# Spectral stage with four input buffers and tables per iteration, hd turned in row pairs, chunk spectra in one block, new memory map and order

## The chip, the cores and the metric

The program runs on one core of one Trainium2 chip. The metric is the device time of one launch in microseconds (us). A core has a matmul engine (PE, whose weight loads are shown as PEld), three engines for other arithmetic (DVE, ACT, POOL), a sync engine (SP) that issues nearly all transfers here, and 16 DMA engines that carry them out. SBUF is the core's memory of 128 partitions; PSUM receives the matmuls' results. Profiles come from one profiled execution, times from several executions without a profile beside it.

## The reference, cut to what matters

Forward and gradient of a block of sequence length S = 2048, width D = 512, inner width F = 1376, in bf16. All outputs are wanted: the output and the gradients of x, k, v, shift_k, ssm_k, ssm_D and the three weight matrices.

```python
xn = layernorm(x)
k_shift = sum over t < 4 of k delayed by t, times shift_k[:, t]
kv = k_shift * v
y = irfft(rfft(kv, 2S) * rfft(ssm_k, 2S))[:S] + kv * ssm_D
out = x + xn * y + ((xn @ w_gate) * (xn @ w_up)) @ w_down
```

With `grad_out` = go, the gradient needs h = g u, and the gradients of g and u, from xn @ w_gate, xn @ w_up and go @ w_down^T. The program calls the three of them hd: they are what is multiplied again by the weights for the output and the gradient of xn.

## The kernel before, in words

Rows are tokens; 128 tokens are a row tile, of which there are R = 16 (r), handled in pairs. The inner width is cut into six blocks j (`SW`: 256 columns, block 1 has 96). The whole order of the instructions is fixed beforehand: the functions only record operations (`Op`), and `emit` (L180) replays them in the order, and with the PSUM slots, that the string `PLAN` holds. Each engine works its own list in that order, so an instruction that waits holds all behind it on the same engine. SP is one such list: a load that waits for memory to come free holds all transfers behind it. All tiles lie in one SBUF tensor, `big`, at addresses written out by hand, so every tile has the name `big` in the profile; all instructions go through the recorder's line L172.

- **Start.** `xload`, `gtload`, `gload` (L326 to L332) bring x, go turned (`goT`) and go. `ln` (L369) makes the LayerNorm of two rows: statistics on DVE, the square root on ACT, reciprocal and scaling on DVE (for some rows on ACT). `tr_rows` (L384) turns xn on PE. Warm-up matmuls without use for the result run first: 8 of 512 columns and 24 of 128.
- **Blocks.** `mlp_rows(j, r)` (L391) makes hd for two row tiles of block j: 24 matmuls, copies from PSUM on ACT or DVE, two products on DVE. The result lies in `ring(j, r)` (L273), a ring of 24 slots of 1,536 bytes for each row tile, with block 1 in the slots 16 to 23 in a form of its own. `dw_gen(j)` (L534) makes the weight gradients of a block from xn, go and the ring: 96 matmuls of 512 columns (block 1: more and narrower ones). `hd_store` (L408) writes hd of four row tiles to DRAM (`HD`), for the blocks 0 to 3, and of block 4 for the rows below `KEEP` = 8.
- **Convolution, forward half.** `a_gen` (L417) makes k_shift (products with `SK` on DVE), kv and xn go, multiplies row tiles by a 64-point table (`W1`) and stores the result to DRAM (`AX`).
- **Spectral middle.** `s_load` (L461) brings pieces of AX back into two buffers `sp["a"]`; `s_B` (L468) multiplies by the table `E`, `s_pw` (L483) forms products of spectra on DVE, `s_Bi` (L500) multiplies by the table `ET` and stores to DRAM (`CX`), in eight iterations. E and ET, 512 KB each, are loaded once (`a_all`, L791).
- **Turning.** The last products need hd with the inner width on the partitions. `hd_load(m)` (L579) reads HD by a transposing DMA, for one row tile m at a time: 640 of its rows for even m, 512 for odd m, and 128 fewer where m is 8 or above. Even row tiles have two buffers `hdE`, odd ones a single `hdO`. What isn't in HD (block 5, and the rows 8 to 15 of block 4) is turned by `turn_gen` (L559): 128x128 transposes on PE, eight to a PSUM slot, and an ACT copy of each slot.
- **Final stage**, in eight chunks n of two row tiles. `c_load` (L613) brings a chunk of CX, `last_dft` (L652) multiplies it by `W2`, `c_dkv`, `c_y`, `c_o5`, `c_dsk`, `dk_pair` make the gradients of v, k, ssm_k and shift_k mostly on DVE. `y_o` (L719) makes the block's output from hd and w_down (11 matmuls of 512 columns a row tile), `y_x` (L732) the gradient of x (22 matmuls and LayerNorm's gradient on DVE). `dkv_load`, `y_load`, `k_load` bring v, k_shift (`KS`), x and k of a chunk. At the end of a chunk two further row tiles of hd are loaded:

```python
            for m in (2 * n + 3, 2 * n + 4):
                if m < 2 * NCH:
                    hd_load(m)
```

Of the kernel before, what the change touches and what calls it, by code (L numbers as in the profile page):

```python
# [29 lines left out]
KEEP = 8  # L30
EPS = 1e-5
PLAN = "c-lpG0~98^?{<;~UE8*8+qP}nwr$(CZQHi(y?1y2@4NSRzHg?JO!M?fnw*|aCpI7e!~uf1kOtyGd`JKe5(0yOLLxBm5CTF%C<qN<AS{G~@DKqaLL`U`Q6MTrgXoYIVn9rY1*IV|WP|Kb268|W$O-wO9^`_gkOy)@eaH(1pfV(bd{7X|LKP?kRUtW)hr&<}ia<3e3dNv06o=-J0xCcWr~x&h7Sx7H&<RpPNoWDRpboTz&d>mQLtUr{sh}0~fkx088bTZB3*Dd{^n=DQ4oX26Xae0~0i=eu&=vYaQy2>EVIcH?W-tsoz`rm6IzmsF0pnpIM8cUc9MZ!em;fVT5sZL|Fc=oYBp3yoVF;v!$uJty!5CNtOCU4Mf+?^Xrovd51505xEQ94R4d%iYSOL>vD`bIruoAYxeAo+XAOmcNeXtI8z*^V^J7GV3hV}3fzQArc02$#RY=k|q0gl2~I0VPx8)SlGa2QU)5jX+g;WC_pi|`xH!Fjj>Kj0EvfYT5U<6{C$h-aV+cEv<^4IaQ%_z8(|6LiCe&>eeVXzYoP;2*dSk0A-3qojBPlHnit1<CO&5T?MCm<m%PVj4_~PvADB!(P}ML*P^BgLj}WJ_o>I_zXtiC+LU6u|JN)QP>zAHo?)@6dA|j7z~BYP;nDB#}?QUL*hefg@&!M4TizC*bdvHU<V9~v#}#~!Z{cYJx<5YI1|I;0GxpXaTX53!8i|ZLIfOwm9R3-#amDiBVuGMgoUvP-i4yL8dqQxya&bbK19XhSOQC8DU61tu?&{Qa#$XtV+E{&Rk0dY#8ns*W8fOBj&X1$*1(#00&8JyT#K==4mO~57#m-}D_D<p@g>y5xY&^D;|6Siuc0B<p+>k7H{%-^iU+YS)uVm*7T&`+d<XSu5`KUQI36csdYp(EFe6UIop=B<;S}73hwuw!#>F@dvtU*{j7u;Z?!oMs1CL-%%!Ru#H|D{km>2WmLfnh_@fdEwMOXj_(tO;8CvhoW!K-);uj388iMMbB-Nrk(AMfHlypIp?AwI&#_ynKgR(yuf@ddub<M;|+;~RX7@9;f-z}oZ?KjCNmf?x3)e#am96aT^O_%Hs#-}nau3xJ3mF$pOdc?v-xDHMgKFcg-;QFw|#3os%@qVu>6n@~Txh!-$2?Z8Xej0R8?DoLfNDV3%&G>FPlIch=8=`s$c<dlL^QYvamsVNPmr6H7#(o+V?NSP=zWudH;jmpzdsz4Q~5@n|xv>bC%E;@z7C^zMys5FoAQa;L01*jkuqLEaXiqLc_O2w!+Ri-LbmHJaPDnY}kI@O?P6rEyFO^QjeC^p5RMsynEQap-J3Fr(?p@fu(5>paNN@uY#b);l8o?6j4>_n}pElr|{)P~yA1nNoCr~|d58PuI7Q!naFqi81epf0qEu2C&oN3&=(eWl*ChQ`ut8bj-;E3KueG@9nn2AWUZXd~^Xy)=&I(gE5{eP|z@r=_%q4$>CtOBZMbEvId?j5g6B+D<F!B5kFgw3#l^zw{67qy==D&d@K~K}YEdEvB=yhz`>++C>ZLJ3XSSbexXR54uAy=>#pI-*l2<x>zo@yHAfPj*IK!xqB4f-K7NX8zpp!Tw?cxlDMQUnfpT_+*1nUPSFDj>DYyJ&jJfT+;eL0PE&H{+zU$KLb;Sq-E|7>I=Jxe26c3uTxWNay0}}^)eUsv+<UrBgIqWFkv>p&*TeO6y<BhiiTb#{uAdv~`n%8ciiWwtE|q&juPL=l<I=ixF1>q88C*t}$z^s!To(6^vbt<;xXbQxxSXz@tM78T2CkuN<Z`>lu8C{vnz`n#g=^_RTDjKl54Uk`U0GMowR7bixI8YeLzmCxcOzT@H_4fc;wC%q3c5%xs*B(vyD2W3i|AOUy6A4S6H$rb#=0@iWSkr6LWq}XZoC`iP^P;I&Iw6espu-Xcv9I_aaG+6SIt#-A*F_^>1w&!u8y1FX1Tg9tW0$CTxgl;R=7|y-z{+~-E6nag_osnj$7`+Nf?PQtK3|-*hP>+E};~5MO;KF>LN)omq3cU$dX7(xFk~2t#(^oR7orgTvFNQO1WfGLQ1>na@{R-#bu2v<D$q7mt1bTMedfn?bf<G?ykG%V#s~>z(tdXE~ccG0WOw2a%ttUd*WitQx`{`xik`*GfNmwC(m72&LZJBgM{Z}?zlVQ(o1%Uz$qk$oOD?wm7H>?T{b!6a>`kkQqH+da^B^VGLl;^xQtR(^2kMZ$>o*H?usiXS6z9@ClUFYi^LmTMS0;0N&#8tDo7#8FaNkA@~_+IN=ji_?|!*b(ou@ZZ}-O)l}-Y@$sv~(;?1sx)RV}(#nqB19F?Q7<GNB)n1w5eas#O%`(1r$B9&#YYb?eGTr;UE`<&;dQe8rDNNy+xT_Xv_&83cPch#hYymW_LH>oW<+$+~oUc2t{#<h~Su8q8N?_CdRE1l)A`{24td->=-xg+kg`{KIDSJzs;xpvZ1zPk?6TV~4-my72}FUiKaxxWmTpDsENkQf}3vvVwt!*O|_jFxyjLUM3y9wa$=jO=tnBoD{u!IFUcNM26JyWA*A#EE&N^phmK+a={>JXVr(UrE8kWUlOSDS5oilcO#ZkCUM?QRYiJ&cK;@f=rc3vRE>5Dqbq7ISZHIX);C9a4}BLOC&ANkWyTdC(A5ZAk(EZFO*}FmGkjYDZ_<$k<66*T!0JnMp-EZxj3(qqFjzwOA)TbTcrY*<;q;1*GNU)B-MDG)ZnVTR<=nkuEI6BIxmyj{EZv%7Fi*6xj!$L0lY&t$Ur_Wb+{q#l0m#)Hp^f>AwzhNwBnO8l()+;9?m1UH6M^uvQJv@PB|loWVeju(=v+B%4j|!E&08S;k`1J&&vlH$NQxox8Z{_o-fNesn6~Bu(an6d__9)9qGiKxeH&Fu6#jmOE<nG-MI%pke=L&@5@E$&G)1a_vO2CO&&=<KEgNTp&aE2e2kCt6FI@x<s?6rTk=Jo$tnIOr}?Iw;j{cy&hb}i#4qHdyp+cLouA8j{v>bY0$=1y{7NqKXKBXo<h6X4E8LW?adZADF*TOHm5JPzf5>mS&XX8)GMi4}2mD7+RUh(Hp2kk6b11#XA+-sU{v-E!2LF-}I+Jg)*D(5TU|X8Sp*6PN=Gh!hS?6$AjiYlpg3jalyny5C4GypIbRqxXoBW6)X?%^WcX%^L(=Ggy6X;e>s8KYAZsW&%UnA;v-oc4=Cr8y?yqov%6HcUiIlAuSB)Xq7Xfi#(2l)^$;-tEm(`zbS!iRY&XVPVSM^o!^&ZsLmo37+loJO~6R$a}>HHYrdyP93s@Ke60Yk3`~)DN6RGixqQq3b!FZs3i)S3mMyPOC3?6X(-?nnz#pRnDm|d8fYSPh3EEX<mKDx%CZy=KNY%|K<1mjEm|Q{>tUFh?du1Tuh&H1udw>b+^9didsnvX$h^YRkWj4)oQv&OKK-At(~=tcGYfLO1o<h?Ww)AtoGJE+E>eHKkcu-d4TTMfjUSB>jAB<HMFMI(%M=_>*^34s`Yf3F43jBOo!_TU9Ky1rLNMax?0!hT3x5>b%Soy-?~XR>uo)#TXeEc(L*{_r|ES4hiB+aou#vNj?UG2I$sy)LS3XIb(AjF(K<%Q>Np**^>u<y)CSs6C+Sgrpj-8rHqwXsSsUwNZKAKWsXozW+FV=cBW<Zi^qIEO*7`=<=yPqWAN0C@)mPe1Z|Gyas_*ose$w`u&(7*cy{2z9k#*27dQQ)4V!Ng9^`c(T@0!G3DBC4XYA;pnhi+3fZ(+>rr-rbw7Slr6WesWJ?27)Q-}IM;xBQmOPU`?WuK#KQJEIXSmc=o$6B^NCTR|&kajm!&vUpa);@e66qa`hYozjFB$-tsoa*J%vQdnq<Vks?}MYmLz+G1E5%WByzt);UJR^D=0ddp}Ptd!-nik90lS!t_ebu61@w)$4t8dw!8Y)!1HHMKHU!&+K3%VI^WmDRPfR@7SCK+9wGtf95Bwl>JBTO%86Bdn%1wjox_Mp}0}XrrvQHM7yy&YD|$>tLO1qD`{N*3mj!PwQe+tgDT&7B<xu*gP9=)2x>*wdvNw#@aILYs+nx&9GIr$X44zTVq3Qt*x+iHq(aLdYf&F?U2o}4c5=*+78=jhi#K>wo7)zF54D6YFq7!?X;`5&92#XyJ5HOt-Z6G*3I5qF1uxSY`A@}?Y7cB+I+ifdF_+kvvT&?mKYlQFZRv8+IRb5y=|90wEOnccH206VK42KowWY;+RoZ3``7l_X}e%i{5d;gQT-E(=AYUli|!v=41dgG`s4P@`dBRg#>DTpxc<4t_UZftQ~%5M*l&yD&BycUeR%JE2LHz*`HVh-Pw3BECLiCEPwDqs0{_60`OyA^IiJ}l^%pIbKVVsWVxQV4@mYNspWTP>VSP4V#3%RRd{rOP=ke8i4iCP%&*>xjGCr3t>dX2xzML=SYxv^6yszm?_*x!)K406X^(lNEpVzna^?U_i*Vp&0d?R1kxAql%e&5cw@r8VQU%+?pp?p*Sk9G7-d^6w4m-L-|bKl1g_6>X&U&?p&-Th=g#ZUD^{50RqH}pgObl<}d^D}%;Khu}?z5E<s*w69>{cxYi_w%#;Hb34+_H%t-zua&4{rx1r!w>R1{Q$qn@A3=$2*2A`@*DjgzsZmEZT)7y*AMi${b;|!AMyMA7C*+X^ke-2zsisE^ZaVR-=FfQ{Tbib&-VxY8b8XP^)37oztEraYkhBj$e;IB{0)EDU-0Yvb-&eL_V@h*f6+hmH~k~O*kAHX{bPT{Kk>KxRlm$X_3QmL|H9w)8~ihW$3OQI{7Zk=zw#6PTmQ~~@E`qAf6O2E_xx-B-oNpm{0aZrpY&!dYHEQau<(EH0j<n|eZg4&vjt9A!V*9r@K*>7q=EL|KntGA0&sw65CAEN2A-h903757N2vYB`zzUkKtKco{Xcu41sH*t9Do8W)nG^qb^=#WG6$i+2lPJ^2Rv)gzXd6Or3B%>LxQe?mjwNBAo_nd2c-t)AIJbSXbC2x6x95`F+l&xzZMQsh&h;eaFYDj!v7;{kQsCpEY{yD1!D)R7f3LWHUG`)Zz2I#!CC!J1(OZvfC?5TVC4Vb3sz4553vrLHv"
# [4 lines left out]
def kernel(  # L37
# [33 lines left out]
    CX = dram.tile([128, 32, 3 * D + 32], BF, name="CX")[:, :, 0:3 * D]  # L71
# [167 lines left out]
    rc = Region(0, 8 * KB)  # L239
    rX = Region(8 * KB, 40 * KB)  # L240
    rT = Region(40 * KB, 72 * KB)
    rW = Region(72 * KB, 96 * KB)
    RH = 96 * KB
    RA = (132 * KB, 207 * KB)

    ident = rc.tile("ident", [128, 128])
    SK = rc.tile("SK", [128, 4, D])
# [5 lines left out]
    Drow = rc.tile("Drow", [128, D])[0:1, :]  # L253
# [8 lines left out]
    std = rc.tile("std", [128, R], F32)  # L262
# [18 lines left out]
    nc.vector.memset(eps_t[:], EPS)  # L281
    ra = Region(*RA)
# [7 lines left out]
    tmpA = ra.tile("tmpA", [128, 2, D])  # L290
    ksH = place([128, 4, D], BF, RA[0])
    E = place([128, 32, 2, 32], BF, RA[0] + 4 * KB)
    ET = place([128, 16, 2, 64], BF, RA[0] + 8 * KB)
# [27 lines left out]
    for i in range(24):  # L321
        now[0] = -40.0 + i
        MM(at0[:, 0:128], lhsT=ones1[:], rhs=ones1[:], start=True, stop=True)
# [5 lines left out]
    def gload(r, n):  # L329
        ld(go[:, r:r + n, :], go_d[:, r:r + n, :])  # L330

# [11 lines left out]
    xload(0, 2); step()  # L343
    ld(Wl[0][:, 1024:3072], w_d[:, 1024:3072]); step()
    xload(2, 2); step()
    gtload(1, 1); step()
    xload(4, 4); step()
    gtload(2, 2); step()
    ld(SK[:].rearrange("p j d -> p (j d)"), bass.AP(tensor=sk_d.tensor, offset=sk_d.offset, ap=[[0, 128], [1, 4 * D]])); step()
    xload(8, 4); step()  # L350
    gtload(4, 2); step()
    xload(12, 4); step()
    gtload(6, 2); step()
# [3 lines left out]
    nc.gpsimd.memset(place([128, 48, 128], BF, RH + 1536 * 16)[:, :, 0:32], 0.0)  # L357
# [11 lines left out]
    def ln(r0, n):  # L369
        for r in range(r0, r0 + n):  # L370
            nc.vector.bn_stats(stats[:, r % 4, :], xn[:, r, :])
            nc.vector.bn_aggr(mv[:, r, :], stats[:, r % 4, :])
        gs = slice(r0, r0 + n)
        nc.scalar.activation(std[:, gs], mv[:, gs, 1], ACTF.Sqrt, bias=eps_t[:, 0:1], scale=1.0)
        nc.vector.reciprocal(rstd[:, gs], std[:, gs])
        if 2 <= r0 <= 8:
            STT(c1[:, r0 + 1:r0 + 2], mv[:, r0 + 1:r0 + 2, 0], -1.0, rstd[:, r0 + 1:r0 + 2], op0=ALU.mult, op1=ALU.mult)
# [140 lines left out]
    def s_gen():  # L518
        for i in range(9):
            if i < 8:  # L520
                if i:
                    s_load(2 * i)
# [472 lines left out]
```

## Time and profile before

| | |
|---|---|
| median of 5 runs | 441.2 us |
| lowest and highest | 439.49 and 446.31 us |
| the profiled execution's own time | 444.49 us |
| its span, first to last instruction | 442.7 us |
| PE busy before 294 us | 284.8 us |
| PE busy from 294 to the end | 138.1 us |
| transposing loads of HD | 16, median 8.5 us from issue to landing |
| loads of CX chunks | 8 of 1,536 KB, median 7.2 us |
| bytes moved by DMA | 124.12 MB |

A row of the profile's groups names the engine, the operation, what it writes and reads, the shape and count, then the busy time of the group in us, the mean of one in ns, and the idle time just before its instructions with what ended it. Busy time of a group is that of its union, so for overlapping matmuls it is less than count times mean. A row of waits has us in total, times, and the longest. The share of DMA is the time that packets took, divided by 16 engines' time; as packets overlap, it can exceed 1.

### The profile page before, as it was taken

The numbers are of one execution on the slowest core, as the hardware profiler recorded it, in microseconds if no ns is written. First come the engines' busy times: TensorE is split into PE (matmuls) and PEld (weight loads), VectorE is DVE, ScalarE is ACT, GpSimd is POOL, SyncE is SP. The second block draws the span as 40 slices with busy tenths as digits, with TensorE's granted clock in tenths as the row PEclk, the third lists the DMA queues.
The fourth block names the chain that finished last, engine by engine and source line by source line (L and its number), as shares of the span: only waits on it lengthen the run. The fifth ranks groups of instructions, "written<-read, shape, count | busy, mean of one in ns | idle before, by whom it ended". The sixth has DMA issues, their size and how long they took to land. (4 is left out here: it accounts for less than half of the span.)

```text
span 442.7 us, 8134 instructions
## 1 busy us (share of the span) xinstructions
PE 423.0 (96%) x3179; PEld 204.0 (46%) x3179; DVE 352.9 (80%) x690; ACT 266.0 (60%) x366; POOL 3.4 (1%) x9
## 2 busy tenths in 40 slices
PE   5999999999999999999999999999999999999895
PEld 3555546655445443334444345454444433443342
DVE  2899477699953899979999995044797969999797
ACT  3686778579562669999999998367333113331211
POOL 1000000000000000000000000100000000000000
PEclk9799999999999999999999999999999999999999
DMA  7988869999947669866587779999999999999992
GB/s 266 408 263 295 309 249 295 351 353 369 359 189 262 224 224 333 269 237 263 178 321 260 292 272 254 283 344 301 325 242 281 289 291 330 250 280 263 241 314 88
DMA packets 96366, 124.12 MB, mean 280 GB/s; under 512 B 53316, under 2 KB 62153, under 8 KB 96328
## 3 DMA queue, kind: packets, MB, share of 16 engines
q1 hardware_dynamic: 96328, 123.60, 87.3%
q8 instruction: 25, 0.41, 0.4%
q14 instruction: 13, 0.11, 0.1%
HBM read 56.57 MB, written 54.04 MB: 250 GB/s over the span
## 5 line engine op out<-in xcount | busy, mean ns | idle before, releaser
L172 PE MATMUL PP<-big 128*128 128x512 bf16 (+8 forms) x3179 | 423.0, 347 | 14.6 <-DMA big<-in_goT_dram 3.8
L172 PEld LDWEIGHTS <-big 128*128 128x128 bf16 (+4 forms) x3179 | 204.0, 98 | 233.1 <-issue 72.0
L172 DVE TENSOR_TENSOR big<-big 128x1024 bf16<-128x1024 bf16 (+5 forms) x465 | 267.9, 634 | 53.1 <-ACT big L172 43.4
L172 ACT CAST big<-PP 128x1024 bf16<-128x1024 f32 (+2 forms) x311 | 224.5, 787 | 93.6 <-PE PP L172 81.5
L172 ACT ACTIVATE big<-big 128x512 bf16<-128x512 f32 (+2 forms) x28 | 18.6, 669 | 71.8 <-DVE big L172 55.0
L172 DVE CAST big<-PP 128x512 bf16<-128x512 f32 (+1 forms) x37 | 32.4, 878 | 13.4 <-PE PP L172 11.4
L172 ACT COPY big<-PP 128x1024 bf16<-128x1024 bf16 x25 | 25.1, 1037 | 5.9 <-PE PP L172 5.9
L172 DVE SCALAR_TENSOR_TENSOR big<-big 128x1 f32<-128x1 f32 (+2 forms) x52 | 25.1, 504 | 0.5
L172 DVE BATCH_NORM_STATS2 big<-big 128x6 f32<-128x512 bf16 x16 | 10.7, 678 | 7.3 <-DMA big<-in_x_dram 7.3
L172 DVE TENSOR_TENSOR big<-big,PP 128x512 bf16<-128x512 bf16 (+1 forms) x17 | 10.9, 656 | 6.9 <-PE PP L172 6.8
L172 DVE SCALAR_TENSOR_TENSOR big<-big,PP 128x512 f32<-128x512 bf16 x16 | 11.0, 686 | 3.0 <-PE PP L172 3.0
L172 DVE TENSOR_SCALAR big<-big 128x1 f32<-128x1 f32 (+1 forms) x28 | 7.0, 263 | 0.2
L172 POOL MEMSET big<- 128x1536 bf16 (+2 forms) x3 | 2.8, 949 | 281.3 <-DMA CX<-big 281.3
L172 ACT ACT_TABLE_LOAD x2 | 2.6, 1283 | 0.8 <-PEq L983 0.7
L172 DVE BATCH_NORM_AGGREGATE big<-big 128x2 f32<-128x6 f32 x16 | 2.6, 174 | 0.1
L172 DVE RECIPROCAL big<-big 128x2 f32<-128x2 f32 x8 | 1.3, 158 | 1.3 <-ACT big L172 1.3
L172 DVE DVE_READ_ACCUMULATOR big<-big 128x1 f32 x16 | 1.4, 87 | 0.0
L172 DVE DVE_READ_ACCUMULATOR big<-big,PP 128x1 f32 x16 | 1.4, 86 | 0.0
L172 DVE COPY big<-PP 128x1024 bf16<-128x1024 bf16 x1 | 0.7, 692 | 0.5 <-PE PP L172 0.5
L172 DVE MEMSET big<- 128x1 f32 (+1 forms) x2 | 0.2, 112 | 0.8 <-PEq L983 0.8
masks.py:199 POOL TENSOR_SCALAR_AFFINE_SELECT big<-big 128x128 bf16<-128x128 bf16 x1 | 0.3, 293 | 0.0
masks.py:197 POOL MEMSET big<- 128x128 bf16 x1 | 0.2, 204 | 0.3 <-POOLq L983 0.3
(4 smaller groups left out, 0.4 us busy)
## 6 DMA issues: line engine op xcount, KB each, us to landing
AX<-big SPq DMA_DIRECT2D x16, 768.0 KB, 4.7
big<-AX SPq DMA_DIRECT2D x16, 768.0 KB, 4.7
CX<-big SPq DMA_DIRECT2D x16, 768.0 KB, 5.3
big<-CX SPq DMA_DIRECT2D x8, 1536.0 KB, 7.2
out_dram<-big SPq DMA_DIRECT2D x44, 256.0 KB, 3.3
HD<-big SPq DMA_DIRECT2D x14, 768.0 KB, 5.6
big<-in_v_dram SPq DMA_DIRECT2D x16, 256.0 KB, 4.5
big<-in_w_dram SPq DMA_DIRECT2D x4, 768.0 KB, 7.8
```

The costliest lines, as they stand in the source:

```text
L172: o.fns.append(lambda: f(*[fix(x) for x in a], **{kk: fix(x) for kk, x in k.items()}))
```

## The change

- **Start.** Sixteen of the 24 small warm-up matmuls go. x comes row by row for the first two rows, goT's second pair comes ahead of the rest of the first weights, and the following loads are cut smaller. The first two rows have a LayerNorm each. A square root without use stands first on ACT. `std` goes: the root is written into `rstd` and inverted in place.
- **shift_k** is loaded twice, to `skA` for `a_gen` and to `skF` for the final stage, in place of one tile that stays.
- **Memory map.** All regions move; block 0 has a ring of its own at 183 KB, and the other blocks share the 24 slots anew.
- **Spectral middle.** Four AX buffers instead of two, all four filled before the first iteration; both tables of an iteration come as one piece of 128 KB a time into three buffers; the CX stores go out in 32 pieces instead of 16.
- **CX** is laid out by chunk, so that a chunk is one block of 12 KB to a partition.
- **hd.** `hd_store` now also stores block 4 for the rows 8 to 15; block 1 moves to the end of a row of HD. `hd_load(n)` turns both row tiles of chunk n by one DMA of 1,152 rows, into one of two buffers, and is recorded at the end of chunk n - 2. `turn_gen` is left with block 5.
- **PLAN** is a new order with new PSUM slots.

```diff
-    for i in range(24):
+    for i in range(8):
...
+    nc.scalar.activation(s1[:, 0:1], eps_t[:], ACTF.Sqrt)
...
 gtload(0, 1); step()
 ld(Wl[0][:, 0:1024], w_d[:, 0:1024]); step()
-    xload(0, 2); step()
+    xload(0, 1); step()
+    xload(1, 1); step()
+    gtload(1, 1); step()
     ld(Wl[0][:, 1024:3072], w_d[:, 1024:3072]); step()
...
-                        ln(0, 2)
+                        ln(0, 1)
+                        ln(1, 1)
...
-            k = (16 * SB[j] + r) % RING
+            k = (16 * SB[j] + 16 + r) % RING
...
+        sp["a"] = [m.tile(f"sa{i}", [128, 2, 3, D]) for i in range(4)]
+        sp["E"] = [m.tile(f"sE{i}", [128, 512]) for i in range(3)]
...
+    def e_load(i):
+        ld(sp["E"][i % 3][:], tab_d[:, 192 + 512 * i:192 + 512 * i + 512])
...
-            dst = CX.rearrange("(g k) r e -> (k r) g e", k=4)[:, 4 * i + 2 * s:4 * i + 2 * s + 2, :]
-            st(dst, sp["C"][s][:].rearrange("p g t d -> p g (t d)"))
+            for g in range(2):
+                st(CX.rearrange("n (g a e) -> g a n e", g=32, a=16)[4 * i + 2 * s + g], sp["C"][s][:, g].rearrange("p t d -> p (t d)"))
...
-                if i:
-                    s_load(2 * i)
-                s_load(2 * i + 1)
                 yield from s_B(i)
+            if i < 6:
+                s_load(2 * i + 4)
+                s_load(2 * i + 5)
             if i >= 1:
                 yield from s_Bi(i - 1)
+                if i < 6:
+                    e_load(i + 2)
...
-        for j, r0 in ((NST - 2, KEEP), (NST - 1, 0)):
+        for j, r0 in ((NST - 1, 0),):
...
-    hdE = [place([128, 6, 640], BF, a) for a in (73 * KB, 86 * KB + 512)]
-    hdO = place([128, 6, 512], BF, 73 * KB + 7680)
-
-    def hd_load(m):
-        a, b = 128 * (m % 2), 640 if m < KEEP else 512
-        ldT(out=(hdO if m % 2 else hdE[m // 2 % 2])[:, :, 0:b - a], in_=HD[m, a:b])
+    hdP = [place([128, 6, 1152], BF, 67 * KB + 13824 * i) for i in range(2)]
+
+    def hd_load(n):
+        ldT(out=hdP[n % 2], in_=HD.rearrange("r p e -> (r p) e")[1280 * n:1280 * n + 1152])
...
     def c_load(n):
-        r0 = 2 * n
-        ld(f["C"].rearrange("q (h r) e -> q h r e", h=2), CX.rearrange("q (h r) e -> q h r e", h=2)[:, :, r0:r0 + 2, :])
+        ld(f["C"].rearrange("p r e -> p (r e)"), CX[n].rearrange("(q e) -> q e", q=128))
...
-                if p % 2 and (j < NST - 2 or j == NST - 2 and 2 * p - 2 < KEEP):
+                if p % 2 and j < NST - 1:
                     hd_store(j, 2 * p - 2)
...
+    sk_load(skF)
...
-            for m in (2 * n + 3, 2 * n + 4):
-                if m < 2 * NCH:
-                    hd_load(m)
+            if n + 2 < NCH:
+                hd_load(n + 2)
```

## The prediction, as it was recorded before the changed kernel ran

> **What bounds the kernel now.** I read the engines' busy time first, then the busy time by stretches, then the waits, then SP's timeline and the DMA queue.
>
> ```profile
> PE 423.0 (96%) x3179; PEld 204.0 (46%) x3179; DVE 352.9 (80%) x690; ACT 266.0 (60%) x366; POOL 3.4 (1%) x9
> ```
>
> The matmul engine is the bound over the whole. The table by stretches (stretch, its length, then busy us and count for PE, PEld, DVE, ACT, POOL; granted clock; DMA share; GB/s) says where it is not:
>
> ```profile
> 3.90:10.70 6.80, 2.97 (x37) 2.39 (x36) 2.51 (x7) 2.16 (x3) 0.00 (x0) 1.00 0.95 323
> 10.70:17.60 6.90, 6.11 (x29) 3.33 (x28) 5.32 (x17) 2.67 (x6) 0.00 (x0) 0.51 1.04 409
> 17.60:40.00 22.40, 21.11 (x161) 13.01 (x160) 20.50 (x55) 20.13 (x35) 0.00 (x0) 1.00 0.90 322
> 150.00:272.00 122.00, 121.90 (x1224) 52.36 (x1223) 116.98 (x215) 109.64 (x139) 0.00 (x0) 1.00 0.76 272
> 294.00:350.00 56.00, 56.00 (x355) 26.76 (x353) 44.49 (x88) 24.07 (x27) 0.00 (x0) 1.00 1.00 290
> 350.00:437.70 87.70, 82.13 (x433) 35.92 (x431) 80.53 (x173) 21.07 (x25) 0.00 (x0) 1.00 1.00 262
> ```
>
> The spectral middle (150 to 272) leaves PE 0.1 us idle. Idle or slow PE time is at the start (3.8 us idle before 10.7, then half clock) and after 350 (5.6 us), where the DMA share is 1.00. The waits, and DVE and PE at the start:
>
> ```profile
> PE PP L172 <- DMA big<-in_goT_dram: 3.8, 1, 3.8
> PEld L172 <- DMA big<-HD: 4.6, 4, 1.5
> PE PP L172 <- DMA big<-CX: 2.5, 2, 1.8
> ...
> 9.79 0.69 DVE L172 BATCH_NORM_STATS2 big<-big 128x6 f32<-128x512 bf16 x1 [2.64 <-DMA big<-in_x_dram]
> 10.40 0.15 DVE L172 RECIPROCAL big<-big 128x2 f32<-128x2 f32 x1
> ```
>
> So two things are late at 10.4: goT of the second row pair, and the reciprocal of the first LayerNorm pair, queued on DVE behind the statistics of row 2, whose x lands at 9.79. For the end I read SP's timeline and the DMA counts of 294 to 430 and of 350 to 360:
>
> ```profile
> 342.09 7.55 SPq L172 DMA_TRANSPOSE big<-HD  x1
> 349.75 0.52 SPq L172 DMA_DIRECT2D big<-in_v_dram  x1
> 350.37 7.72 SPq L172 DMA_TRANSPOSE big<-HD  x2
> 358.14 3.44 SPq L172 DMA_DIRECT2D out_dram<-big  x6
> ...
> DMA packets 55510, 38.33 MB, mean 282 GB/s; under 512 B 43861, under 2 KB 43989, under 8 KB 55501
> ...
> DMA packets 7667, 2.33 MB, mean 233 GB/s; under 512 B 7457, under 2 KB 7457, under 8 KB 7666
> ```
>
> SP is held 3 to 8.5 us by each transposing load, and stores pile up behind. Of these loads' bytes every 256 make a packet: six per HD row. Where they run alone (350 to 360) 7,457 packets took the 10 us, so **746 packets per us**.
>
> **What the Trainium skill says.** "TensorE: Matmul & The Clock Gate", section "What's actually happening": idle windows of about 3.4 us halve the clock. The trace agrees: 44% busy up to 10.7, then 0.51 for 6.9 us. Same page, "Wait — 56ns, not 53.3ns?": 55.6 ns from one 128-column matmul to the next, 215.7 ns for 512 columns; 278 to 284 holds some 28 of the latter in 6.00 us, 0.21 each. "DMA: Bandwidth & Descriptors", "Latency and other measured facts": 261 GB/s for transposing DMA; the trace's 746 packets make 191 GB/s, and the trace's figure is used. "ScalarE: Activation LUTs", "What ACT_TABLE_LOAD costs": 1,283 ns and a drain of 1,380; the trace shows 1,283 and no drain after it.
>
> **The start.** goT's second pair moves ahead of 512 KB of weights and 256 KB of x: 768 KB at 252 to 323 GB/s is 2.4 to 3.1 us earlier than 10.41. The first two rows get LayerNorms of their own, the square-root table loads before data, and both rows stand on DVE ahead of row 2; the pair was ready at 11.31 and can be at about 7.9 (x landed by 6.2; statistics 0.87, root 0.29, reciprocal 0.15, scaling 0.41, hand-overs). That frees 3.4 us, and up to 2.8 more if the clock holds (three us of matmuls ran at half rate). But DVE then sets the pace: 20.50 of 22.40 us busy up to 40, its LayerNorms done at 35.3. Its instruction order in the changed kernel has three more products of a_gen ahead of the last LayerNorm (3 x 0.69 = 2.0 us), against the 2.64 us block, some 0.7 us of earlier x and about 1 us of small idle times that go. So **-2.0 us**, from 0 to -5. The 16 small warm-up matmuls that go (107 ns at the half clock) stood in the wait for goT: nothing, or a cold clock if the cover they gave is needed, 2.8 us at most.
>
> **The turning of hd.** Block 4's rows 8 to 15 are no longer turned on PE: 48 of 144 transposes and 6 of 18 ACT copies (1,037 ns each, 6.2 us).
>
> ```profile
> L172 PE MATMUL PP<-big 128*128 128x128 bf16 x232 | 17.7, 224 | 0.3 <-ACT big L172 0.3
> ```
>
> 17.7/232 is 76 ns with the cold warm-ups in it, 56 by the skill: 2.7 to 3.7, I take 64 ns, **-3.1 us**, PE being the bound there. ACT's part is worth nothing: it waits for PE or DVE. In exchange two more HD stores (1.57 MB, PE busy and DMA share 0.76 in that stage: hidden), and the transposing loads grow from 49,152 to 8 x 1,152 x 6 = 55,296 packets, all 6,144 more in pairs 4 to 7: **8.2 us of DMA time** where the share is 1.00. The second load of shift_k, 0.5 MB at 290 GB/s, adds 1.8. Against these 10 us: the last mlp_rows, which frees the memory of the first hd_load, stands 3.4 us of matmuls earlier (counted in the order of instructions), with the start 5.4. The remaining 4.6 us meet a queue with some 5% of slack. I take half as reaching PE: **+2.3 us**, from -5 (late PE waits vanish) to +13 (below).
>
> **The pairs.** hd_load(n+2) waits until both rows of pair n are read. What follows on SP waits with it: the chunk loads v, KS, x, k, CX and all stores; for these wait DVE (c_dkv, c_y) and ACT (the store of o1 frees f["t"]). Between release and first use PE has 12 to 17 us of matmuls; the shortest is hd_load(5), 44 matmuls of y_x/y_o, one last_dft, two c_dsk: 11.7 us. A pair needs 6,912/746 = 9.3 us alone.
>
> **The rest.** Four AX buffers, tables per iteration (8 loads for 2), 32 CX stores for 16 (some 0.4 us of SP each, 6.4 in 120 us): PE has no wait there to lose, so nothing; if SP's queue delays AX loads, up to +2. CX in one block per chunk moves the same bytes. The first last_dft waited 0.7 us for CX (2.5 less the 1.8 of another chunk); from the last spectral matmul to it PE now has 17.1 us of work, before 16.9. Inside that time lie two ACT copies (2.0), four CX stores (about 2), their landing (5.3 on the page), and c_load(0) (7.2): 16.5, if SP is free. hd_load(0) stands ahead of these stores on SP and now carries two rows: one row held SP 6.45 us there, a pair may hold it 13, from a start some 8 us before the ACT copies end. So -0.7 to +4, taken as **-0.7**, since this load also starts earlier. The memory map lets block 2 start before block 1 is done: no PE wait there to remove. DVE's sum changes by one small LayerNorm operation; the tail after the last matmul (437.7 to 442.7) has the same operations: 0.
>
> **Sum.** -2.0 - 3.1 + 2.3 - 0.7 = -3.5 on a span of 442.7. That execution's own time was 444.5, 3.3 above the median 441.2 of the five; the difference carries over: 437.7, and as the unknowns of the start lean downward, **437**.
>
> **Rivals.** A, the sum above: 433 to 441, 0.45. B, **the pairs arrive in time**: with whole double buffers and earlier release the 5.6 us of idle PE after 350 goes, and the clock holds at the start: -4 - 3.1 - 5 = -12, 429. For it: 294 to 350 already runs at 56.00 of 56 with pairs of full size; against: that stretch was fed by work loaded ahead. 0.24. C, **the DMA queue becomes the bound**, slower: per pair 9.3 us of transposing plus 3.93 MB of plain traffic (CX 1.57, nine pieces of 0.26) at 358 to 409 GB/s (the rates at 360 to 370 and at 10.7 to 17.6), 10 to 11; 20 us, /1.05 for the overlap seen in the share, 19.3, against 17.1 of PE; over six pairs +13 less the gains of 5.8: 448. It decides once a pair's transposing load takes longer than the PE work between release and use. For it: the share of 1.00 and the waits on HD; against: that the queue is measured with overlaps, and stores can slip past the last load. 0.2. D, **the start gains nothing** because DVE paces it, and the DMA eats the transposes: 441, 0.11.
>
> **Numbers.** About 1% (4.4 us) is what I count as told from no change. A gives faster 0.22 and same 0.23, B faster 0.24, C slower 0.19 and same 0.01, D same 0.11: faster 0.46, same 0.35, slower 0.19. The range 429 to 447 holds A, most of B and part of C.
>
> **What would show it.** First mlp_rows of pair two near 7.5 and clock 1.00 at 10.7 to 17.6 for the start; 168 instead of 232 matmuls of 128 columns (48 transposes and 16 warm-ups less); SP held 7 to 16 us by each of eight transposing loads; PE's waits on HD after 350 below 4 us (B), about 9 (A), above 15 (C). I am wrong if PE waits in the spectral stage, or if last_dft of chunk 0 starts later than 289.

## The result and the profile after

The changed kernel takes **440.82 us** (median of 31 runs, 437.43 to 442.38) beside 442.59 us for the kernel before in the same sitting (52 runs). The ratio is **0.9948** with a 95% interval of 0.9933 to 0.9964: 2.3 us less, half a per cent (1.8 us by the two medians). Run twice more beside the experiments it gave 0.9926 [0.9903, 0.9948] and 0.9945 [0.9925, 0.9966]. The prediction was 437 with a range of 429 to 447, a fall of 4.2 us from the median of 441.2 that it started from, and the largest share of its chance (0.46) lay on "faster" by about 1% or more. The time lies inside the range; the fall is about half of the forecast one.

The profiled execution has a span of 438.2 us (its own time 440.25), 4.5 less than the 442.7 of before; that one ran 1.9 us above its kernel's median, this one 0.6 below, so that 2.5 of the 4.5 us lie in the choice of executions. First the busy time by engine, then the stretches of time that were shown of before, and with them 40 to 150 (stretch, length, busy us and count for PE, PEld, DVE, ACT, POOL; granted clock; DMA share; GB/s):

```profile
PE 420.9 (96%) x3115; PEld 201.1 (46%) x3115; DVE 351.1 (80%) x691; ACT 260.0 (59%) x361; POOL 3.4 (1%) x9
```
```profile
3.90:10.70 6.80, 4.78 (x34) 3.44 (x32) 2.60 (x9) 1.65 (x4) 0.00 (x0) 0.81 0.95 280
10.70:17.60 6.90, 4.26 (x30) 2.25 (x29) 6.90 (x22) 4.39 (x8) 0.00 (x0) 0.94 1.04 406
17.60:40.00 22.40, 22.12 (x186) 14.31 (x185) 21.86 (x58) 19.21 (x37) 0.00 (x0) 1.00 1.01 387
40.00:150.00 110.00, 110.00 (x839) 58.09 (x838) 84.27 (x138) 76.44 (x119) 0.00 (x0) 1.00 0.87 307
150.00:272.00 122.00, 122.00 (x1172) 51.58 (x1171) 108.47 (x201) 106.53 (x135) 1.41 (x2) 1.00 0.85 278
294.00:350.00 56.00, 55.40 (x301) 24.95 (x299) 42.03 (x87) 18.86 (x21) 0.00 (x0) 0.97 1.12 283
350.00:437.70 87.70, 80.16 (x418) 34.93 (x416) 79.87 (x173) 20.73 (x24) 0.00 (x0) 0.98 0.96 275
```

Before, the fourth of these stretches read:

```profile
40.00:150.00 110.00, 108.67 (x813) 58.92 (x812) 79.50 (x132) 73.44 (x119) 0.00 (x0) 1.00 0.81 290
```

Three things are to be seen. From 10.7 to 17.6 DVE is the busy engine (6.90 of 6.90) and PE is not (4.26); from 17.6 to 40 both are nearly full (DVE 21.86, PE 22.12 of 22.40). The 1.3 us that PE idled between 40 and 150 are gone. And the last stage, for which three of the prediction's terms were meant, still leaves PE idle, and now also at half clock; its DMA share rose from 1.00 to 1.12 up to 350 and fell from 1.00 to 0.96 after it. What PE waits for has changed, though (total, times, longest):

```profile
PE PP L171 <- DVE big L171: 5.7, 7, 1.5
PE PP L171 <- ACT big L171: 3.7, 7, 1.2
PE PP L171 <- DMA big<-in_goT_dram: 2.0, 1, 2.0
PE PP L171 <- DMA big<-CX: 1.0, 1, 1.0
```

The waits on HD (4.6 us before) are gone, and waits on DVE and ACT stand in their place. By marks in the order of PE's instructions, the first block's mlp_rows end at 37.6 us (39.9 before), last_dft(0) starts at 287.4 (291.9), and the last matmul ends at 433.3 (437.6). So 2.3 us come from the start (by its end the new order has also done 12 matmuls of block 1, some 0.7 us), 2.2 from there to last_dft(0), 1.3 of them the idle time between 40 and 150, and the last stage, from last_dft(0) to the last matmul, takes 145.9 us where it took 145.7. It returned nothing for 3 us of PE work less.

These 3 us are not simply the 48 transposes. In the order of before 56 transposes of the turning stood ahead of last_dft(0) and 88 behind it; now 16 and 80 do. Only 8 of the 48 left the last stage. In the place of the other 40 stand 13 matmuls of the weight gradient (some 0.21 us each) that came behind last_dft(0) before. So the saving of the turning reaches the last stage by way of other work moved ahead: 13 matmuls, 2.8 us, and 8 transposes.

The last stage's two places of loss, on DVE, SP and PE (start, us, engine, what, idle before and its releaser):

```profile
332.93 10.85 SPq L171 DMA_TRANSPOSE big<-HD  x1
...
347.27 0.42 SPq L171 DMA_DIRECT2D big<-KS  x1
```
```profile
351.92 0.15 DVE L171 TENSOR_SCALAR big<-big 128x1 f32<-128x1 f32 x1
355.59 2.67 DVE L171 TENSOR_TENSOR big<-big 128x1024 bf16<-128x1024 bf16 x4 [3.52 <-DMA big<-KS]
```
```profile
292.80 0.62 PE L171 MATMUL PP<-big 128*32 128x512 bf16 x8 [1.22 <-ACT big L171]
293.72 0.61 PE L171 MATMUL PP<-big 128*128 128x128 bf16 x8 [0.30 <-ACT big L171]
294.63 5.53 PE L171 MATMUL PP<-big 128*128 128x512 bf16 x23 [0.31 <-ACT big L171]
...
360.78 0.41 PE L171 MATMUL PP<-big 128*64 128x512 bf16 x2 [1.46 <-DVE big L171]
362.08 6.16 PE L171 MATMUL PP<-big 128*128 128x512 bf16 x20 [0.89 <-DVE big L171]
```

At 293 PE waits for ACT, which has nine PSUM copies of about 1 us in a row from 288, six of them of turning groups. At 355 DVE waits for KS of chunk 3, which SP issued at 347 behind a transposing load that held it 10.85 us; then PE waits for DVE to free PSUM. After each of the two places the clock is halved for 3.4 us:

```profile
291.38:294.79 3.41, 1.58 (x21) 0.91 (x19) 3.41 (x6) 3.41 (x5) 0.00 (x0) 1.00 1.00 310
294.79:298.20 3.41, 3.41 (x9) 1.18 (x8) 0.27 (x1) 1.63 (x2) 0.00 (x0) 0.50 1.22 267
359.65:363.06 3.41, 1.39 (x7) 0.68 (x7) 3.07 (x10) 2.90 (x4) 0.00 (x0) 1.00 1.24 313
363.06:366.47 3.41, 3.41 (x10) 1.18 (x8) 3.38 (x6) 1.45 (x2) 0.00 (x0) 0.50 0.95 282
```

### The profile page after: what moved, and what is told of

It is laid out like the page before. It is cut to its first block, busy times and chain, and to the rows that moved or that the text cites. A ratio compares the mean times of both kernels' runs of the same rounds, so it can differ in the third digit from the quotient of the medians.

```text
span 438.2 us, 8056 instructions
## 1 busy us (share of the span) xinstructions
PE 420.9 (96%) x3115; PEld 201.1 (46%) x3115; DVE 351.1 (80%) x691; ACT 260.0 (59%) x361; POOL 3.4 (1%) x9
## 4 chain that ended last, share of the span: by engine, by line
PE 71%; DVE 18%; DMA 4%; ACT 3%; issue 2%; SPq 1%; DVEq 0%; ACTq 0%
PE PP L171 71%; DVE big L171 18%; ACT big L171 3%; DMA out_dram<-big 2%; DMA big<-in_x_dram 2%; SPq L171 1%; DVEq L1008 0%; DVEq L171 0%; ACTq L171 0%
## 5 line engine op out<-in xcount | busy, mean ns | idle before, releaser
L171 PEld LDWEIGHTS <-big 128*128 128x128 bf16 (+4 forms) x3115 | 201.1, 98 | 231.9 <-issue 74.1
L171 ACT ACTIVATE big<-big 128x512 bf16<-128x512 f32 (+3 forms) x30 | 19.0, 641 | 82.8 <-DVE big L171 67.1
L171 ACT COPY big<-PP 128x1024 bf16<-128x1024 bf16 x19 | 19.0, 1030 | 8.0 <-PE PP L171 8.0
L171 DVE RECIPROCAL big<-big 128x2 f32<-128x2 f32 (+1 forms) x9 | 1.4, 156 | 0.4 <-ACT big L171 0.4
```

The costliest lines, as they stand in the source:

```text
L171: o.fns.append(lambda: f(*[fix(x) for x in a], **{kk: fix(x) for kk, x in k.items()}))
```

## The experiments

Theories at the outset: **SP hold** (the transposing load delays KS, so DVE, so PE), **DMA volume** (the prediction's own: the queue is full), **ACT burst** (the copies of the turning groups behind last_dft(0)); later **half clock** and **coupled resources**. In the diffs, `after(a, b)` moves an instruction b of PLAN's order to stand right behind a. All kernels start from the changed one. "Clock" is the mean over the runs of the granted clock.

| run | ratio to before [95%] | median us | clock |
|---|---|---|---|
| the changed kernel | 0.9948 [0.9933, 0.9964] | 440.82 | 0.992 |
| e1_again, e17_third (the same) | 0.9926 [0.9903, 0.9948], 0.9945 [0.9925, 0.9966] | 438.59, 440.01 | 0.993, 0.991 |
| e2_ks2 | 0.9927 [0.9904, 0.9950] | 439.27 | 0.994 |
| e3_turn | 0.9975 [0.9952, 0.9999] | 441.83 | 0.988 |
| e4_both | 0.9961 [0.9935, 0.9987] | 440.96 | 0.989 |
| e5_hd896 | 0.9944 [0.9921, 0.9966] | 439.86 | 0.991 |
| e6_turn2 | 0.9950 [0.9925, 0.9974] | 439.98 | 0.996 |
| e7_dve | 0.9922 [0.9889, 0.9956] | 439.21 | 0.991 |
| e8_ks2dk | 0.9912 [0.9877, 0.9946] | 438.79 | 0.996 |
| e9_fill | 0.9936 [0.9913, 0.9959] | 440.42 | 0.993 |
| e10_start | 1.0012 [0.9991, 1.0033] | 443.25 | 0.984 |
| e11_warm | 0.9935 [0.9912, 0.9958] | 439.38 | 0.996 |
| e12_poolq | 1.0737 [1.0680, 1.0793] | 477.70 | 0.952 |
| e13_best_dve | 0.9908 [0.9880, 0.9937] | 438.75 | 0.994 |
| e14_best_hd896 | 0.9903 [0.9869, 0.9936] | 438.51 | 0.996 |
| e15_all | 0.9869 [0.9834, 0.9905] | 436.21 | 0.992 |
| e16_all_turn2 | 0.9882 [0.9854, 0.9911] | 436.55 | 0.996 |
| e18_candidate | 0.9913 [0.9880, 0.9946] | 439.19 | 0.995 |

**The two places, one at a time (e1 to e4).**

```diff
-            ld(f["ks"][:], KS[:, rs, :])
+            ld(f["ks"][n % 2][:], KS[:, rs, :])
...
+    for n in (3, 4, 5):
+        after(("v", n), ("ks", n))
```

> The changed kernel once more, with the same instructions on every engine, as the common mark for the three runs beside it. Expected: 0.993 to 0.997 of the kernel before; from last_dft(0) to the last matmul again about 145.9 us, with the PE held by DVE for 1.76 and 0.89 us about last_dft(4) and by ACT for 1.2 us about 293, each followed by a stretch of half clock.

> A second buffer for the shifted-k rows KS, and the KS loads of chunks 3, 4 and 5 issued right behind the v load of the same chunk, so that KS(3) leaves SP at about 325 and no longer at 347 behind the transposing load of chunk 3. Nothing else moves. Theory 'SP hold' (the gain of the turning was given back because that load holds SP 10.9 us and KS comes late): DVE's wait of 3.5 us on KS at 355 goes, PE's waits of 1.76 and 0.89 us and the half clock of 363.1 to 366.5 go with it: 3 to 4.5 us less than the changed kernel. Theory 'DMA volume' (the transposing loads fill the queue): at most 0.5 us less, since the bytes are the same and the wait comes back on another load. Theory 'ACT burst' says nothing of this place: at most 1 us less if DVE is late anyway.

```diff
+    for p, q, k, b in ((1643, 1644, 80, 6), (1830, 1791, 72, 7), (1835, 1858, 88, 7), (1838, 1859, 40, 7), (1894, 1890, 64, 6)):
+        after(p, ("turn", k))
+        after(q, ("turned", k))
```

> Five of the turning groups that PE does between last_dft(0) and y_o(0,0) are moved: one into PE's idle microsecond ahead of last_dft(0), four behind the first two y_o and y_x of row 1, where ACT has nothing to do. Same instructions, other places. Theory 'ACT burst' (ten copies of 1.02 us in a row on ACT hold PE after last_dft(0), and the half clock follows): PE's waits of about 3 us between 286 and 295 go, and the half clock of 294.8 to 298.2: 3 to 4 us less than the changed kernel. Theory 'SP hold': the time gained there is lost again at KS of chunk 3, which SP issues no earlier: 0 to 1.5 us less.

> Both edits, the second KS buffer and the moved turning groups. If the two places are separate and each is what its theory says: 6 to 8 us less than the changed kernel, about 433 us. If one wait only takes the place of another (DVE or the transposing loads are late next): 2 to 4 us less.

In e3 and e4 the copies of groups 72 and 40 came to stand ahead of their transposes, so that these two of the twelve groups hold old data; the instructions are the same in number. None of the three gained: e2 is level with e1 beside it, and e3 is even slower than it, by 2.2 us. Most of that goes with its clock, the lowest of the four: at 3.3 us for each 0.01, the slope found below, its 0.0055 less would make 1.8 us. DVE in e2 shows why nothing was gained there:

```profile
352.83 1.28 DVE L173 TENSOR_TENSOR big<-big 128x1024 bf16<-128x1024 bf16 x2
357.81 1.29 DVE L173 TENSOR_TENSOR big<-big 128x1024 bf16<-128x1024 bf16 x2 [3.69 <-DMA out_dram<-big]
```

KS is there, and DVE waits 3.69 us for the next thing on its list, the store that frees the accumulator of the k gradient. In e3 PE stands 1.6 us on ACT and then 2.1 on DVE, before c_dsk(0): the edit moved the wait and did not remove it. "SP hold" named its wait rightly and its price wrongly; "ACT burst" named its wait rightly, and e3 leaves the price open.

**One resource at a time (e5 to e8).**

```diff
-        ldT(out=hdP[n % 2], in_=HD.rearrange("r p e -> (r p) e")[1280 * n:1280 * n + 1152])
+        m = 1152 if n < 4 else 896
+        ldT(out=hdP[n % 2][:, :, 0:m], in_=HD.rearrange("r p e -> (r p) e")[1280 * n:1280 * n + m])
```

> The changed kernel with the transposing loads of chunks 4 to 7 cut from 1,152 to 896 rows of HD, the volume that the kernel before moved there: 6,144 packets of 256 bytes less, 8.2 us of the queue by the rate seen. It leaves out four blocks of every second row pair half of these chunks, so the outputs of the GLU are incomplete; PE, DVE and ACT do the same work. Theory 'DMA volume' (the queue is full from 294 to 400, share 1.06 to 1.15, so that every load and store waits longer and DVE and PE with them): 2.5 to 5 us less than the changed kernel. Theory 'order' (SP's and DVE's in-order queues set the end, whatever the volume): at most 1 us less.

```diff
+                for i, (r, t, b) in list(enumerate(blk[k:k + 8])) * (2 if k in (0, 8, 16, 24, 48, 56) else 1):
```

> The changed kernel with six of its twelve turning groups done twice on PE (48 transposes more, 3.1 us at 64 ns, which is the number that the change took away); nothing else differs. If PE's work sets the time there, as the prediction's term of -3.1 us has it: 2.5 to 3.5 us more than the changed kernel. If PE has slack in this stage, because DVE or the queue is the bound: at most 1 us more, and the term bought nothing.

```diff
+            if j == 3:
+                drop.extend((len(ops), len(ops) + 1))
             TT(dst[:], dks_rows(r0 + j), skb(skF, j, 2), op=ALU.mult)
```

> The changed kernel without the last tap of the gradient of k: 16 DVE instructions of 0.69 us less (11 us of DVE), so this gradient is incomplete; loads, stores and PE's work stay. Theory 'DVE is the bound of the last stage' (25.00 us busy of 25 between 375 and 400): 4 to 9 us less than the changed kernel. Theory 'DMA volume': at most 1.5 us less, since every load and store is still there. Theory 'PE is the bound': at most 1.5 us less.

```diff
+    after(("dka", 2, 3), ("dk", 4, 0))
+    after(("dka", 4, 3), ("dk", 6, 0))
```

> The second KS buffer again, and on DVE the first product of the k gradient of rows 4 and of rows 6 placed behind the sums of the pair before, since in the run with the second buffer DVE stood 3.69 us at 354 on the store of that gradient's buffer instead of on KS. Theory 'order': DVE's waits of 3.7 us at 354 and of 2 us at 338 go and nothing is late next: 2.5 to 4 us less than the changed kernel. Theory 'DMA volume': the wait takes another place again, at most 1 us less.

The intervals of all four overlap those of the changed kernel's own three sittings. 8.2 us of the packet queue less and 11 us of DVE less bought nothing that can be told, and 3.1 us of PE more cost nothing that the time shows. But e6 ran at a mean clock of 0.996 where the changed kernel's three sittings have 0.992, which by the slope of 3.3 us for 0.01 is worth some 1.2 us: at one clock the transposes were not free. In e8, which is e2 with these two moves on DVE, DVE's wait at 354 and PE's at 360 are gone, and PE waits for CX and HD instead:

```profile
PE PP L173 <- DMA big<-CX: 1.8, 2, 1.6
...
PE PP L173 <- DMA big<-HD: 1.2, 1, 1.2
```

**The last stage taken apart.** From the trace's PE instructions: the stage's length, PE's waits in it (those over 60 ns), its half-clocked time, and what is left when the waits and half of the half-clocked time are taken off. Where waits lie inside a half-clocked stretch this takes off too much, most in e3.

| run | stage | waits | half clock | left |
|---|---|---|---|---|
| before | 145.7 | 5.5 | 0.0 | 140.2 |
| changed | 145.9 | 5.4 | 6.8 | 137.1 |
| e1 | 144.4 | 5.9 | 3.4 | 136.8 |
| e17 | 147.4 | 6.6 | 6.8 | 137.4 |
| e2 | 145.1 | 7.3 | 0.0 | 137.8 |
| e3 | 147.5 | 7.3 | 10.2 | 135.1 |
| e4 | 145.8 | 7.2 | 6.8 | 135.2 |
| e5 | 146.4 | 6.3 | 6.8 | 136.7 |
| e6 | 146.0 | 6.4 | 0.0 | 139.6 |
| e7 | 147.1 | 7.2 | 6.8 | 136.5 |
| e8 | 144.7 | 6.8 | 0.0 | 137.9 |
| e9 | 147.4 | 8.7 | 3.4 | 137.0 |
| e10 | 144.9 | 6.0 | 3.4 | 137.2 |
| e11 | 144.9 | 6.9 | 0.0 | 138.0 |
| e13 | 145.5 | 6.7 | 3.4 | 137.1 |
| e14 | 144.0 | 5.7 | 3.4 | 136.6 |
| e15 | 142.0 | 4.1 | 3.4 | 136.2 |
| e16 | 142.3 | 4.1 | 0.0 | 138.2 |
| e18 | 143.4 | 4.1 | 3.4 | 137.7 |

"Left" falls by 3.1 us from before to changed, for the 13 matmuls and 8 transposes named above, and rises by 2.5 in e6, of whose 48 extra transposes 32 (2.0 us at the prediction's price) lie in this stage. So PE's work counts in this sum with about its price, and waits and half clock make up for it.

Five of the traces have the changed kernel's own instructions in this stage: changed, e1, e17, e10 and e11. On average they have 6.2 us of waits (0.1 of them where matmul records are missing) and 4.1 us at half clock, where the one trace of before has 5.5 and none. Against 2.9 us less in "left" that is 0.7 us more of waits and 2.0 us of PE's time lost to the clock: on these traces the half clock is the larger part of what was given back.

**Filling the place behind last_dft(0), and the start (e9 to e11).** e9 is e8 and this:

```diff
+    for p, q, k, b in ((1643, 1644, 80, 6), (None, 1774, 72, 7), (1830, 1816, 88, 7), (1835, 1858, 40, 7), (1838, 1860, 32, 7), (1894, 1890, 64, 6)):
...
+    for n, i in enumerate((1798, 1799, 1800, 1807)):
+        tags["early", n] = i
+    after(1767, *[("early", n) for n in range(4)])
```

The first loop moves turning groups, the second y_o(0, 0) and the first part of y_x(0, 0), which now stand ahead of c_dsk(0). In e10 the second goT load goes behind the weights and x rows 2 and 3, the Sqrt table's load behind the first LN's root:

> The second KS buffer and the later first products of the run before, and now also the place behind last_dft(0) refilled: one turning group ahead of last_dft(0), y_o of row 0 and the start of y_x of row 0 ahead of the first c_dsk, and four turning groups where ACT is idle, so that PE has work while ACT copies. Theory 'half clock' (what the change gains is taken back by stretches of 3.4 us at half clock, which come about 2 us after PE has stood for some 1.2 us; 1.7 us of PE each): PE's wait of 1.2 us at 293 goes, the mean granted clock is 0.996 or more, and the time is 3 to 5 us less than that of the changed kernel. Theory 'coupled queues' (whatever is freed is lost at the next wait of DVE or the queue): 0 to 1.5 us less.

```diff
+    tags["goT1"], tags["table"] = 17, 2
+    after(19, "goT1")
+    after(44, "table")
```

> The changed kernel with two pieces of its start undone: the second goT load goes behind the rest of the weights and x rows 2 and 3, and the Sqrt table is loaded at the first LN instead of ahead of it. The prediction's start term says 2.0 us more than the changed kernel (1.3 us of table load at the first LN and 2 to 3 us of goT, partly beside each other), with the start half clocked as before. Theory 'LN on DVE paces the start': 0 to 0.7 us more, since goT is then late where DVE is late anyway.

```diff
+    for k, p, n in ((0, 12, 26), (1, 52, 14)):
...
+            MM(at0[:, 0:128], lhsT=ones1[:], rhs=ones1[:], start=True, stop=True)
```

> The changed kernel with 40 unused matmuls of 128 columns[...] in two waits of PE at the start: 26 ahead of the mlp_rows of pair two and 14 behind the first tr_rows. They do nothing but keep PE busy where it stands 2.0 and 1.2 us. Theory 'half clock follows PE waits': the half clock between 8 and 18 us is seen less often, the mean granted clock rises by 0.003 to 0.006, and the time is 1 to 2 us less than that of the changed kernel. If the half clock does not answer to PE's waits: the same time, or up to 0.5 us more.

In e9 PE's wait at 293 is gone, and 2.3 us of waiting on DVE appear at 312, where c_dsk(1) needs DVE, with the half clock right behind; the time is level with the changed kernel's (0.9936):

```profile
311.07:314.48 3.41, 1.53 (x15) 0.86 (x16) 2.42 (x6) 0.09 (x1) 0.00 (x0) 1.00 1.05 401
314.48:317.89 3.41, 3.41 (x15) 1.17 (x12) 3.38 (x9) 2.68 (x3) 0.00 (x0) 0.50 1.24 168
```

e10 undoes the gain: 1.0012, with an interval that touches none of the changed kernel's. In its trace PE stands 4.6 us on goT, 10.2 us of the start run at half clock, and the first block ends at 42.3 us instead of 37.6:

```profile
PE PP L173 <- DMA big<-in_goT_dram: 4.6, 1, 4.6
```

That is 2.4 us later than before's 39.9; why isn't separated. So e10 shows that the new order needs the two loads early, both together, and not what they won against the kernel before. In e11 the clock was 1.00 in both stretches of the start:

```profile
3.90:10.70 6.80, 5.88 (x71) 4.94 (x70) 2.59 (x8) 1.65 (x4) 0.00 (x0) 1.00 0.96 307
10.70:17.60 6.90, 4.46 (x33) 2.43 (x32) 6.88 (x22) 4.38 (x8) 0.00 (x0) 1.00 1.04 404
```

and the first block still ends at 37.6. So the half clock at the start of the changed kernel's own trace, from 8.07 to 11.49, cost nothing that this mark shows, and e11's time, 0.9935, is level with the changed kernel's. It is not so in every execution. The other traces but e10's have the same start (e11's with the unused matmuls): without half clock their first block ends at 36.8 to 38.2 us, with one such window near 8.3 at 37.6 and 38.6 (e12, e16), with one at 11.6 to 12.9 at 38.3 to 38.9 (e3, e8, e17), and with two at 39.4 and 40.0 (e5, e4).

**Another queue (e12).**

```diff
+        (ld if n < 2 else nc.gpsimd.dma_start)(f["C"].rearrange("p r e -> (p r e)"), ...
```

> The changed kernel with the plain loads of chunks 2 to 7 in the last stage (CX, KS, v, x, k) issued from POOL's queue, which is idle there, and no longer from SP's behind the transposing loads. Theory 'SP hold': KS(3) can leave as soon as its buffer is free (337 instead of 347), DVE's wait of 3.5 us at 355 goes, and the loads of the later chunks are never late: 2 to 4 us less than the changed kernel. Theory 'DMA volume': the queue of packets is as full as before, so that the loads land no earlier than now: at most 1 us less. If issuing from POOL costs more than on SP, the loads are later than now: up to 5 us more.

7.4% slower, further than any theory said: two of the transposing loads beside them took far longer than elsewhere.

```profile
310.43 21.43 SPq L173 DMA_TRANSPOSE big<-HD  x1
...
379.26 32.38 SPq L173 DMA_TRANSPOSE big<-HD  x1
```

PE stood 32.0 us on HD, 23.4 of them at one place. So the run can't tell whether SP's hold was the limit.

**Several resources at once (e13 to e16).** These are e9 with the cuts of e7 and e5 alone and together, and with e6's transposes on top. The k gradient lacks its last tap in e13, e15 and e16, and its rows 0 and 1 are overwritten before their store.

> The run with the refilled place, the second KS buffer and the later first products, now also without the last tap of the k gradient (16 DVE instructions, 11 us of DVE; this output is incomplete). Each of the two edits alone changed the time by 1 us or less. Theory 'coupled resources' (PE, DVE and the packet queue are each some per cent from being the bound of the last stage, so that one relieved gives its time to the next): 1.5 to 4 us less than the run without this cut, and DVE's waits no longer hold PE. Theory 'PE alone bounds the last stage, less its half clock': 0 to 1 us less.

> The same run with the transposing loads of chunks 4 to 7 cut to 896 rows instead (8.2 us of the packet queue; part of the GLU is incomplete), and DVE's work whole. Theory 'coupled resources': PE's waits on CX and HD (1 to 2 us each at 364, 372 and 408) go, 1.5 to 4 us less than the run without this cut. Theory 'PE alone': 0 to 1 us less.

> All of it: the refilled place, the second KS buffer, the later first products, 11 us of DVE less and 8.2 us of the packet queue less. Theory 'coupled resources': more than either cut brings alone, 4 to 8 us less than the changed kernel; PE stands under 3 us in the whole stage. Theory 'PE alone': 1 to 2 us less, the time of the changed kernel at full clock.

> All of it, with six of the turning groups done twice on PE (3.1 us of PE), which cost the changed kernel 0 to 1 us. Theory 'coupled resources': with DVE and the queue relieved PE is the bound, and the same 48 transposes now cost 2 to 3.5 us more than the run beside it. Theory 'PE work has its cover elsewhere': again 0 to 1 us.

Here is the first version that stands clear of the changed kernel, e15 at 0.9869 [0.9834, 0.9905]: its interval lies below two of that kernel's three and touches the third at the edge. PE's waits in the stage fall to 4.1 us and the stage to 142.0 (e18 below has the same 4.1 us of waits in its trace without any cut). Either cut alone, on the same base, gave about half (0.9908 and 0.9903, not separable from e9). By the ratios the two cuts simply add up: 0.0028 and 0.0033 less than e9 alone, 0.0067 together. That needs no coupling. Brought to one clock by the slope of 3.3 us for 0.01, the mean spans are 0.2 and 0.8 us less alone and 3.3 us together, but from six to nineteen runs each. So "coupled resources" (PE, DVE and the queue each stand close behind the other) has some support and isn't shown. e16 has only 0.6 us more than e15 by the ratios, at a mean clock of 0.996 against 0.992; at one clock it has 2.0 us more, and "left" rises by 2.0 us, both the price of the 32 transposes.

**A version to keep (e17, e18).** e18 is e8 and e11 together, every output whole; e17 is the changed kernel on the same chip.

> The changed kernel a third time, as the mark for the run beside it: 0.993 to 0.995 of the kernel before, mean granted clock 0.991 to 0.993.

> The changed kernel with the edits that did no harm one by one and kept every output whole: the second KS buffer with KS issued behind v, the first products of the k gradient behind the sums of the pair before, and the 40 unused matmuls in PE's two waits at the start. If the second KS buffer and the later products are worth what their run showed, and the unused matmuls keep the clock: 1 to 2.5 us less than the run beside it, mean granted clock 0.995 or more. If these differences were scatter: within 0.8 us of it.

440.01 and 439.19 us: 0.8 us less, with intervals that overlap (0.9945 and 0.9913). It is no slower, and it can't be said to be faster than the changed kernel.

## Why the prediction came out as it did

- **Start, -2.0: right in size, its share of the time open.** The two traces differ by 2.3 us at the end of the first block (the second pair's mlp_rows at 8.08 us, 7.5 foreseen), and DVE paces the start up to 17.6, as foreseen. That the clock would hold did not come true in the profiled run (0.81 and 0.94), and e11 shows that this did not matter there. But the one trace of before has 6.8 us at half clock just there, and with the new start two such windows went with a first block at 39.4 and 40.0 us (e5, e4), about the old 39.9. Of the 199 runs of before that list a clock, 106 have 0.997 or more; 6.8 us at half clock alone would take 0.008 off. So how much of the 2.3 us other executions share isn't shown.
- **Warm-up matmuls, 0: right.** e11 put 40 unused ones into two waits at the start, and the first block ended at 37.6 as without them.
- **Spectral middle and memory map, 0: wrong for the stretch before it.** "PE has no wait there to lose" was read from 150 to 272. From 40 to 150 PE idled 1.3 us (108.67 of 110), 0.9 of it behind ACT, which waited 1.8 us at 80.8 for an AX store late on SP:

```profile
80.83 3.29 ACT L172 CAST big<-PP 128x1024 bf16<-128x1024 f32 x5 [1.82 <-DMA AX<-big]
81.89 9.69 PE L172 MATMUL PP<-big 128*128 128x512 bf16 x86 [0.87 <-ACT big L172]
```

  The new order has none of it. Of the 2.2 us by which last_dft(0) gained on the end of the first block, the other 0.9 isn't separated.
- **Turning, -3.1: right as work, worth nothing as time.** There are 168 matmuls of 128 columns, as foreseen. Over the whole program PE's busy time, with its half-clocked part counted half, falls from 419.9 to 416.1 us; some 1.0 of that are the warm-ups, so the 48 transposes come to about 2.9, by estimate. (The 76 ns were misread: the 24 warm-ups ran in 1.50 us, not cold; a group of eight transposes takes 0.61 us, the end of its last one included.) **The step that failed is "PE being the bound there", with no term for half clock in the last stage.** Work moved up into the place of 40 of the transposes, and the saving had to show in the last stage. That stage isn't bound by PE's work alone: before, PE was busy for 82.13 of its 87.70 us after 350. Its 5.5 us of waits (2.0 on HD, 1.8 on CX) became 5.4 (3.4 on DVE, 2.1 on ACT), and 6.8 us now ran at half clock, 3.4 us of PE's time. So 137.1 + 5.4 + 3.4 took the place of 140.2 + 5.5, and 145.9 us of 145.7. The new waits are no longer but stand closer together: on the clock's grid (last section) the stage's emptiest window before was 63% busy and the clock held, and the two of the changed kernel that were 41 and 46% busy, shown above, were followed by half clock. Before:

```profile
406.69:410.10 3.41, 2.16 (x10) 0.89 (x9) 3.39 (x9) 0.81 (x1) 0.00 (x0) 1.00 1.22 232
```

  e6, with 32 more transposes in this stage, took no more time, at a higher clock.
- **Transfers, +2.3: the size of the give-back was near by luck, its way was another.** The queue did get fuller (share 1.12, 58,943 packets between 294 and 430 against 55,510), and SP was held 8.0 to 11.8 us by each load, as foreseen. But PE's waits on HD went to none where about 9 us were expected. The late transfer was KS, the prediction's list of "what follows on SP waits with it", which reached PE by way of DVE; and in e5, with the added volume taken away again, no time came back that can be told.
- **First last_dft, -0.7: off by 0.9.** Its wait for CX went from 0.75 to 0.98 us.
- **Half clock: not in the sum for this stage.** Over the runs the mean clock is 0.992 for the changed kernel (76 runs) and 0.995 for before (199): 0.34% of some 440 us, at most 1.5 us more of lost clock per run. Within the changed kernel's runs the span grows by 3.3 us for each 0.01 of clock lost (correlation -0.62). Set beside runs of before with a like clock, in bands of 0.004 from 0.985 up, the changed kernel's median span is 3.0 to 4.8 us shorter (the highest band has only three of its runs), where all runs together give 3.0. So at one clock the fall is about as large as the sum of the terms or larger. That rests on a correlation: no run set the clock of the last stage by itself.
- **The base.** Five runs gave 441.2; 52 gave 442.6. 1.4 us of the distance from 437 to 440.8 is that, and 0.7 the lean "downward", for which no row of the profile spoke. The rest, 1.7 us, is the sum: -3.5 against -1.8 by the medians (-2.3 by the ratio).

Rival B's mark (waits on HD under 4 us) came true without its time: PE waited for DVE and ACT instead. Rival C's did not: PE's waits on HD were gone, and relieving the queue by 8 us had no effect that can be told. What stays open is how the last stage goes in other executions of before, of which one trace is on record, and how far DVE and the queue are coupled.

## What to carry to other kernels

A wait in the profile is worth its length only if nothing else is due just behind it: before pricing it, look at what DVE, ACT and the queues would be waiting for when it is gone, and relieve those together. A single profile of each kernel is too little for 1%: the same last stage took 144.4 to 147.4 us in five. With three resources over 90% busy in a stage, measure such a change with twenty runs of each kernel and look at the granted clock beside the time.

## What the hardware did that I had not expected

- **The half clock goes by a fixed grid of 3.41 us.** The Trainium skill, "TensorE: Matmul & The Clock Gate", section "What's actually happening", says that the window runs free and that an idle window halves the clock. The traces agree on the grid and on the free phase, but the window needn't be idle: of the windows at full clock in the twenty traces, each in which PE was busy for less than 41% of the 3.41 us was followed by 3.41 us at half clock, none above 48% was, and between the two it went both ways (some traces lack a few matmul records, so that PE may have been busier there). The same wait of 1.2 us at 293, in the same order of PE's instructions there, fell into one window in the changed kernel (1.58 of 3.41 us busy, shown above, then 0.50) and was split better in e6:

```profile
290.80:294.21 3.41, 1.88 (x31) 1.38 (x29) 3.41 (x5) 3.41 (x5) 0.00 (x0) 1.00 0.97 316
294.21:297.62 3.41, 3.05 (x19) 1.65 (x20) 1.33 (x3) 2.69 (x3) 0.00 (x0) 1.00 0.93 245
```

  With a phase that differs from run to run, the same last stage has none, one or two such windows in the five traces named above; the spread of 437 to 442 us goes in part with the clock. Where PE is the bound a window costs up to 1.7 us, half of its length.
- **Loads from POOL's queue beside a transposing load.** In e12 two such loads held SP for 21.4 and 32.4 us, where the changed kernel's take 8 to 12, while the core moved 160 GB/s between 379 and 413 us. Why isn't known.
